# Attention's sum over eight keys: three additions on VectorE, or one strided reduction

## The chip, the cores and the metric

The kernel runs on one core of a Trainium2 chip. The metric is the device time of one execution in microseconds; beside the times stands the profile of one execution, with every instruction's start and duration. The engines are called by their names in the profile: PE (TensorE, matrix products; PEld is its loading of weights), DVE (VectorE), ACT (ScalarE), POOL (GpSimd) and SP (SyncE, which here issues transfers).

## What is computed

The input x has 2048 rows of 576 numbers in f32. Its normalized rows go through two branches, and the sum of both and of x is the output.

```python
xn = layernorm(x)
out = x + attention(xn, wqkv, wo) + ffn(xn, w1, b1, w2, b2)

# attention: 32 heads of 18 numbers; query s sees the 8 keys s, s-2, ..., s-14
logits = einsum("bhsd,bhswd->bhsw", q, kg) * 18**-0.5    # positions before 0 are masked
attn = softmax(logits)
o = einsum("bhsw,bhswd->bhsd", attn, vg)                 # the sum over w, the eight keys
return o.reshape(B, S, D) @ wo

# ffn, hidden width 4608
h = relu(xn @ w1 + b1) ** 2
return h @ w2 + b2
```

The change concerns the line marked "the sum over w".

## The kernel before, in words

The 2048 rows are four blocks b of 512 (`TB`), and in a block partition p holds the four neighbouring rows 4p to 4p + 3, called j. The 32 heads are four groups g of eight heads, so a group has 8 x 18 = 144 columns (`CG`).

PE carries most of the time. Its products are made exact enough by splitting each f32 operand in a high half, which ACT writes, and a low half, which DVE writes as the difference. The first product of the feed-forward part takes two blocks at a time and saves products by sums and differences of quarters of the matrices (slots T1, B11, B12 and so on). It is `ffn_pair` (lines 638 to 818), 18 pairs for each half s of the rows. Between its products PE does the second product of the pair before (`add`, line 557, with weights in the tiles w2s). In a pair, DVE adds a PSUM bank and an SBUF tile at lines 772 and 792, and PE goes on in the same bank `bc` after that.

The order of the work is: QKV products for the first rows, `phase_a(0)` (the pairs of blocks 0 and 1, and the second product of block 0), `phase_b0` (the second product of block 1, then the QKV products of blocks 2 and 3 by `quad_step`, whose `row` copies a PSUM bank by ACT and adds a second one by DVE, line 1105), `phase_a(1)` and `phase_b1` (the second product of the last block). In the phases b, DVE makes one low half of a w2 tile (`w2_lo`, line 538) for every 14 matmuls of PE; three tiles of w2s go round, and ACT (`w2_hi`, line 530) fills one when PE has done with it.

Attention has no phase of its own. `attention(b, g)` (lines 384 to 426) is a generator: one pass for each of the 16 pairs (b, g), cut in pieces by `yield`. `side(k)` (lines 430 to 445) runs the next k pieces, and the code above calls it at places that were put there by hand, so the order of DVE's instructions is fixed when the kernel is built. Each engine works through its own instructions in that order, whatever the times are.

A pass has keys k and values v as tiles with a halo of 14 earlier rows, so that the eight keys of row j are eight runs of 144 numbers, two rows apart (`shifted`, line 349). For each of the four j it multiplies q by the eight shifted keys into the tile `pr` (128 partitions, 8 x 144 numbers, line 391) and sums over 18 numbers of a head (line 395). Then come the softmax (lines 398 to 408) and, for each j, the second half: line 414 multiplies the weights by the shifted values into `pr`, a `yield`, and lines 417 to 419 sum `pr` over the eight keys into row j of the tile q, which is free by then. After the last j, POOL issues eight transfers of the rows to DRAM (line 424), and `release` (line 425) lets the next loads of keys and values go. `regroup` (line 884) later reads the rows back, and `o_hi` (line 903) transposes them on DVE for the product with wo.

Helpers record under their own line: every DVE operation of `tt` has L118, so the groups are told apart by tile and shape.

Of the kernel before, what the change touches and what calls it, by code (L numbers as in the profile page):

```python
# [12 lines left out]
ALU = mybir.AluOpType  # L13
ET = mybir.EngineType
AX = mybir.AxisListType
# [35 lines left out]
def block_kernel(ctx: ExitStack, tc: tile.TileContext, x, xt, wqkv, wo, w1, b1, w2, b2, w1l, out):  # L51
    nc = tc.nc
# [12 lines left out]
    def kv_tile(n):  # L65
# [25 lines left out]
                            axis=AX.XY, op=ALU.add)  # L91
# [25 lines left out]
    def tt(out, a, b, op):  # L117
        return nc.vector.tensor_tensor(out=out, in0=a, in1=b, op=op)  # L118
# [230 lines left out]
    def shifted(t, j, *dims):  # L349
        a = t[:, j:j + 1, 0:1]  # L350
        return bass.AP(tensor=a.tensor, offset=a.offset, ap=[a.ap[0], [DIL * CG, W], *dims])
# [19 lines left out]
    def release():  # L371
        free[0] += 1
        fetch()

    def offer(b, g=None):
        if g is None:
            loads.append(("x", b, None))
            queue.append((("x", b), lambda: statistics(b)))
        else:
            loads.extend([("k", b, g), ("v", b, g)])  # L380
            queue.append((("k", b, g), lambda: attention(b, g)))
        fetch()

    def attention(b, g):
        k, q = landed.pop(("k", b, g)), landed.pop(("q", b, g))
        lg = sb.tile([P, NA, W], F32, name="lg")
        mx = sb.tile([P, NA], F32, name="mx")
        sm = sb.tile([P, NA], F32, name="sm")
        for j in range(NJ):
            pr = sb.tile([P, W, CG], F32, name="pr")  # L390
            tt(pr, q[:, j:j + 1].to_broadcast([P, W, CG]), shifted(k, j, [1, CG]), ALU.mult)
            if j == NJ - 1:
                release()
            yield
            nc.vector.tensor_reduce(out=lg[:, j * HG:(j + 1) * HG].rearrange("p a w -> p w a"),  # L395
                                    in_=pr.rearrange("p w (a d) -> p w a d", d=DH), axis=AX.X, op=ALU.add)
            yield
        if b == 0:
            l4 = lg[:4].rearrange("p (j h) w -> p j h w", j=NJ)
            tt(l4, l4, mask[:4, :, None].to_broadcast([4, NJ, HG, W]), ALU.add)  # L400
        nc.vector.tensor_reduce(out=mx, in_=lg, axis=AX.X, op=ALU.max)
        tt(lg, lg, mx[:, :, None].to_broadcast([P, NA, W]), ALU.subtract)
        yield "exp"
        nc.scalar.activation(lg, lg, AF.Exp, scale=SCALE)
        yield
        nc.vector.tensor_reduce(out=sm, in_=lg, axis=AX.X, op=ALU.add)
        nc.vector.reciprocal(sm, sm)
        tt(lg, lg, sm[:, :, None].to_broadcast([P, NA, W]), ALU.mult)
        yield
        v = landed.pop(("v", b, g))  # L410
        for j in range(NJ):
            pr = sb.tile([P, W, CG], F32, name="pr")
            at = lg[:, j * HG:(j + 1) * HG].rearrange("p a w -> p w a")
            tt(pr.rearrange("p w (a d) -> p w a d", d=DH), at[:, :, :, None].to_broadcast([P, W, HG, DH]),
               shifted(v, j, [DH, HG], [1, DH]), ALU.mult)
            yield
            tt(pr[:, :4], pr[:, :4], pr[:, 4:], ALU.add)
            tt(pr[:, :2], pr[:, :2], pr[:, 2:4], ALU.add)
            tt(q[:, j], pr[:, 0], pr[:, 1], ALU.add)
            if j == NJ - 1:  # L420
                for k, (a, z) in enumerate(OPART):
                    rows = oscr[b, k][g * L:(g + 1) * L].rearrange("l (j i) c -> l i j c", i=G)
                    for i in range(G):
                        nc.gpsimd.dma_start(rows[:, i], q[i * L:(i + 1) * L, :, a:z])  # L424
                release()
            yield
# [1373 lines left out]
```

## Time and profile before

| what | value |
|---|---|
| median of 3 runs | 1105.33 us (1104.26 to 1106.77) |
| profiled execution | 1104.88 us |
| its span, first to last instruction | 1103.2 us |
| granted PE clock | 1.000 |
| PE busy | 1091.4 us (99%) |
| DVE busy | 889.3 us (81%) |
| ACT busy | 566.5 us (51%) |

The profile's page gives the busy time of each engine, the chain of work that ended last (followed back from the last instruction, at each step to what released it), and groups of instructions: line, engine, operation, output and input tiles, partitions x elements, count, then the total busy time in us, the mean of one in ns, and the engine's idle time before them. The views asked of the trace are such groups for a window, the waits of an engine, the chain in order of time, and the timeline: start, duration (several equal ones that follow each other are merged, "x2"), engine, line and operation, and in brackets the engine's idle time and what ended it.

### The profile page before, as it was taken

The page shows a single profiled execution, that of the slowest core. Times are in us where ns is not written, and L with a number is a line of the kernel's source. Part 1 is how long each engine was busy: PE and PEld are TensorE (multiplying, and loading weights), DVE is VectorE, ACT ScalarE, POOL GpSimd, SP SyncE. Part 2 cuts the span into 40 slices and gives each one's busy share as a digit, 9 for nine tenths or more (in the row PEclk, how much of TensorE's full clock was granted, in tenths as well). Part 3 has the DMA queues.
Part 4 walks back from the last instruction along what each step waited for, and adds up shares of the span by engine and source line. Part 5 has one row for each costly group of instructions (what it writes and reads, how often), then busy time and mean ns, then how long its engine had stood idle before and what let it go on. Part 6 is the DMA issues. An engine that isn't in the chain of part 4 may idle for free.

```text
span 1103.2 us, 13965 instructions
## 1 busy us (share of the span) xinstructions
PE 1091.4 (99%) x4919; PEld 918.8 (83%) x4919; DVE 889.3 (81%) x1197; ACT 566.5 (51%) x801; POOL 156.8 (14%) x284
## 2 busy tenths in 40 slices
PE   9999999999999999999999999999999999999998
PEld 7998888888888888888899887888888888888887
DVE  7996888999988979989899285776867676889955
ACT  5555655666656564555344354454554545543432
POOL 4011220212130100003010300202101010101010
PEclk9999999999999999999999999999999999999999
DMA  8768998897898697876865988868686877685582
GB/s 275 260 210 294 307 362 305 315 379 275 316 349 297 227 383 245 289 241 226 311 193 164 314 307 278 283 239 320 216 308 209 295 236 301 227 282 190 184 284 87
DMA packets 106549, 297.32 MB, mean 270 GB/s; under 512 B 12784, under 2 KB 39664, under 8 KB 95728
## 3 DMA queue, kind: packets, MB, share of 16 engines
q1 hardware_dynamic: 69104, 188.26, 49.1%
q0 software_dynamic: 14272, 67.24, 17.2%
q10 hardware_dynamic: 23104, 40.94, 11.1%
q8 instruction: 38, 0.62, 0.2%
q14 instruction: 31, 0.25, 0.1%
HBM read 211.90 MB, written 84.49 MB: 269 GB/s over the span
## 4 chain that ended last, share of the span: by engine, by line
PE 88%; DVE 6%; DMA 2%; issue 2%; ACT 1%; ACTq 1%; POOL 0%; DVEq 0%; POOLq 0%
PE p L557 45%; PE p L661 34%; PE p L1093 4%; DVE pr L118 2%; DMA w1s<-w 1%; PE p L1465 1%; PE p L1555 1%; PE p L1097 1%; DVE h L118 1%; DMA out<-h 1%; PE p L667 1%; PE p L1610 1%; DVE r L118 0%; PE p L1382 0%; DVE w1s L118 0%
## 5 line engine op out<-in xcount | busy, mean ns | idle before, releaser
L557 PE MATMUL p<-h,w2s 128*128 128x512 f32 x2066 | 491.9, 389 | 0.0
L557 PEld LDWEIGHTS p<-h,w2s 128*128 128x128 f32 x2066 | 387.6, 188 | 81.7 <-ACT h L708 0.5
L661 PE MATMUL p<-X,w1s 128*128 128x512 f32 x864 | 219.3, 389 | 0.0
L530 ACT ACTIVATE w2s<-w2r 128x640 fp32r<-128x640 f32 x164 | 120.3, 736 | 139.4 <-PE p L557 108.1
L661 PEld LDWEIGHTS p<-X,w1s 128*128 128x128 f32 x864 | 162.2, 188 | 33.7
L118 DVE TENSOR_TENSOR w2s<-w2r,w2s 128x576 fp32r<-128x576 f32 (+1 forms) x165 | 124.0, 752 | 77.2 <-ACT w2s L530 77.1
L661 PE MATMUL p<-S,w1s 128*128 128x512 f32 x648 | 164.8, 390 | 1.4 <-ACT r L746 1.4
L661 PEld LDWEIGHTS p<-S,w1s 128*128 128x128 f32 x648 | 121.5, 188 | 27.2 <-ACT r L746 1.8
L424 POOL DMA_DIRECT2D o<-q x128 | 69.5, 613 | 422.9 <-DVE q L118 421.8
L704 ACT ACTIVATE r<-r,b1t 128x512 f32<-128x512 f32 x72 | 52.2, 724 | 116.3 <-DVE r L118 113.6
L118 DVE TENSOR_TENSOR pr<-lg,kv 128x1152 f32<-128x1152 f32 x64 | 86.7, 1355 | 1.1
L395 DVE TENSOR_REDUCE lg<-pr 128x64 f32<-128x1152 f32 x64 | 86.5, 1351 | 1.2
L118 DVE TENSOR_TENSOR pr<-q,kv 128x1152 f32<-128x1152 f32 x64 | 86.7, 1354 | 0.9
L118 DVE TENSOR_TENSOR r<-p,r 128x512 f32<-128x512 f32 (+1 forms) x77 | 53.1, 690 | 35.5 <-ACT r L770 17.3
L118 DVE TENSOR_TENSOR pr<-pr 128x576 f32<-128x576 f32 (+1 forms) x128 | 77.6, 606 | 3.3
L712 ACT ACTIVATE r<-r 128x1024 f32<-128x1024 f32 x72 | 76.1, 1056 | 1.2
L746 ACT ACTIVATE r<-p 128x512 f32<-128x512 f32 x36 | 21.5, 598 | 84.2 <-PE p L661 81.1
L118 DVE TENSOR_TENSOR h<-r,h 128x1024 fp32r<-128x1024 f32 (+2 forms) x43 | 49.8, 1162 | 13.4 <-ACT r L712 9.6
L118 DVE TENSOR_TENSOR w1s<-w1r,w1s 128x1024 fp32r<-128x1024 f32 (+2 forms) x42 | 46.3, 1103 | 8.7 <-ACT w1s L495 8.2
L704 ACT ACTIVATE r<-p,b1t 128x512 f32<-128x512 f32 x72 | 48.2, 671 | 0.4 <-DMA out<-r 0.4
L118 DVE TENSOR_TENSOR h<-h 128x1024 fp32r<-128x1024 f32 x36 | 43.9, 1220 | 1.7 <-ACT h L989 1.5
L557 PE MATMUL p<-w1s,w2s 128*128 128x512 f32 x195 | 44.7, 389 | 0.0
(227 smaller groups left out, 1185.1 us busy)
## 6 DMA issues: line engine op xcount, KB each, us to landing
w2r<-in_w SPq DMA_DIRECT2D x144, 320.0 KB, 3.7
kv<-kvq POOLq DMA_DIRECT2D x32, 1296.0 KB, 8.2
w<-w1s SPq DMA_DIRECT2D x21, 1024.0 KB, 6.6
w1s<-w ACTq DMA_DIRECT2D x19, 1024.0 KB, 6.2
h<-r SPq DMA_DIRECT2D x36, 512.0 KB, 6.1
h<-h SPq DMA_DIRECT2D x36, 512.0 KB, 4.3
w<-w1s SPq DMA_DIRECT2D x15, 768.0 KB, 9.6
w1s<-w ACTq DMA_DIRECT2D x15, 768.0 KB, 5.6
```

What stands on the lines that cost most here:

```text
L118: return nc.vector.tensor_tensor(out=out, in0=a, in1=b, op=op)
L395: nc.vector.tensor_reduce(out=lg[:, j * HG:(j + 1) * HG].rearrange("p a w -> p w a"), in_=pr.rearrange("p w (a d) -> p w a d", d=DH), axis ...
L424: nc.gpsimd.dma_start(rows[:, i], q[i * L:(i + 1) * L, :, a:z])
L530: nc.scalar.activation(w2s[stream[i]][:, :DE], raw2[i], AF.Copy)
L557: nc.tensor.matmul(yp[b][c], v, a, start=c not in yb[b], stop=c in last and c not in [o[0] for o in ops[i + 1:]], skip_group_check=True)
L661: nc.tensor.matmul(to, l, r, start=start and i == 0, stop=i == len(mm) - 1, skip_group_check=True)
L667: nc.tensor.matmul(to, weight(LEFT, k, f), v, start=False, stop=k == 1, skip_group_check=True)
L704: nc.scalar.activation(to, a, AF.Relu, bias=b1t[:, f:f + 1])
L712: nc.scalar.activation(r, r, AF.Square)
L746: nc.scalar.activation(u[:, 0], bb, AF.Copy)
L1093: nc.tensor.matmul(to, l[:, js], r, start=start and n == 0, stop=n == len(mm) - 1, skip_group_check=True)
L1097: nc.tensor.matmul(to, v[:, js], ws[LEFT, f][:, n], start=False, stop=n == 1, skip_group_check=True)
```

## The change

Three additions that halve the eight keys, 8 to 4 to 2 to 1, become one reduction. It reads `pr` with the keys innermost: for each of the 144 columns the eight numbers that lie 144 words apart. The output is the same row of q. The pieces, the calls of `side` and all other instructions stay in their order.

```diff
             tt(pr.rearrange("p w (a d) -> p w a d", d=DH), at[:, :, :, None].to_broadcast([P, W, HG, DH]),
                shifted(v, j, [DH, HG], [1, DH]), ALU.mult)
             yield
-            tt(pr[:, :4], pr[:, :4], pr[:, 4:], ALU.add)
-            tt(pr[:, :2], pr[:, :2], pr[:, 2:4], ALU.add)
-            tt(q[:, j], pr[:, 0], pr[:, 1], ALU.add)
+            nc.vector.tensor_reduce(out=q[:, j], in_=pr.rearrange("p w c -> p c w"), axis=AX.X, op=ALU.add)
             if j == NJ - 1:
```

## Prediction

> **What bounds the kernel now.** I read first the page's head and its chain of work, then the waits of TensorE (PE), then VectorE's (DVE's) groups by shape.
>
> ```profile
> span 1103.2 us, 13965 instructions
> PE 1091.4 (99%) x4919; PEld 918.8 (83%) x4919; DVE 889.3 (81%) x1197; ACT 566.5 (51%) x801; POOL 156.8 (14%) x284
> PE 88%; DVE 6%; DMA 2%; issue 2%; ACT 1%; ACTq 1%; POOL 0%; DVEq 0%; POOLq 0%
> ```
>
> PE is busy for 1091.4 of 1103.2 us, so at most 11.8 us can be won anywhere. DVE, whose work is changed, is on 6% of the chain that ended last. A cheaper DVE pays only where PE waits for it; a dearer one is free until it has used up the time by which DVE runs ahead of PE, and from there each microsecond counts. So the question has two parts: what one strided sum costs, and how far ahead of PE DVE is at each place where the sums stand. Of PE's waits, one lies behind DVE's attention work:
>
> ```profile
> PE p L1093 <- ACT kv L1103: 0.9, 1, 0.9
> ```
>
> **What is removed and added.** There are 64 sums (16 passes of attention by 4 rows). Rows of DVE's groups by shape (busy us, mean ns of one | idle before):
>
> ```profile
> L118 DVE TENSOR_TENSOR pr<-pr 128x576 f32<-128x576 f32 x64 | 48.3, 754 | 1.1
> L118 DVE TENSOR_TENSOR pr<-pr 128x288 f32<-128x288 f32 x64 | 29.3, 458 | 2.2
> L118 DVE TENSOR_TENSOR q<-pr 128x144 f32<-128x144 f32 x64 | 19.7, 308 | 2.2
> L395 DVE TENSOR_REDUCE lg<-pr 128x64 f32<-128x1152 f32 x64 | 86.5, 1351 | 1.2
> L401 DVE TENSOR_REDUCE mx<-lg 128x32 f32<-128x256 f32 x16 | 6.7, 416 | 0.3
> L933 DVE TENSOR_SCALAR r<-r,flip 128x512 f32<-128x512 f32 x4 | 1.9, 486 | 3.0 <-ACT r L925 3.0
> ```
>
> Removed: 754 + 458 + 308 ns, and 2.2/64 us, or 34 ns, of idle before each of the last two: 1588 ns a sum, 101.6 us in all. Added: one TENSOR_REDUCE that reads 1152 elements and writes 144. L395 reads as many, in order, in 1351 ns; L401 has the new groups of eight, in order, at 416 ns for 256. Between the two rows an element costs (1351 - 416)/896 = 1.044 ns and an instruction 149 ns.
>
> What no row shows is the order of the reads: in the new sum successive elements lie 144 words apart, and no operand of DVE in this trace steps so. **Lower end**: the order costs nothing, 1351 ns as L395. Below that I see no way, since every element is still read. **Upper end**: each element takes two turns, 149 + 1152 x 2.088 = 2554 ns. **My value**: L933 takes its contiguous words at (486 - 149)/512 = 0.658 ns each, so words that lie side by side can come in together. I assume that a word without a neighbour behind it wastes such an access, and charge every element one on top of its own 1.044: 149 + 1152 x 1.702 = 2109 ns. That is an assumption. I take it because L395, the lower end, has neighbours throughout and the new sum has none, so the lower row is the one that is far. With d for what a sum adds to DVE's time: d = -0.24 us at the lower end, 0.52 at my value, 0.97 at the upper end.
>
> The row of L395 alone would make the change a gain. [...]
>
> **Where a dearer sum reaches PE.** DVE works in program order; behind a longer sum stand its other jobs: freeing PSUM banks, and the low halves of weights. A lag grows by d with every sum and is gone when DVE next waits for PE.
>
> Place 1, the first of the QKV products of phase b0, in the chain of waits (start us, us, what):
>
> ```profile
> 541.59 1.36 DVE h L969 x2
> ...
> 550.14 0.77 DVE pr L118
> ...
> 554.73 0.68 DVE pr L118
> ...
> 558.05 0.77 DVE pr L118
> ...
> 561.62 0.77 DVE pr L118
> ...
> 572.95 1.06 DVE w1r L118
> ...
> 574.03 0.02 ACT w1s L1025
> ...
> 574.87 0.52 ACT kv L1103
> ```
>
> From 541.59 to the weights at 572.95 the chain is DVE's; four sums stand in it (a row each for their first addition). ACT's split of these weights, and its copy at 574.87 behind it in its queue, hold PE: this is the wait of 0.9 us above. No room is left, so **4d = 2.08 us**.
>
> Place 2, the pair of phase a0 at 176 to 190 us (start, duration, engine):
>
> ```profile
> 175.89 1.25 DVE L118 TENSOR_TENSOR pr<-pr 128x576 f32<-128x576 f32 x2
> 181.61 1.25 DVE L118 TENSOR_TENSOR pr<-pr 128x576 f32<-128x576 f32 x2
> 184.64 1.25 DVE L118 TENSOR_TENSOR pr<-pr 128x576 f32<-128x576 f32 x2
> 188.62 0.69 DVE L118 TENSOR_TENSOR r<-p,r 128x512 f32<-128x512 f32 x1
> 189.61 1.52 PE L661 MATMUL p<-X,w1s 128*128 128x512 f32 x6
> ```
>
> Line 772 reads bank bc until 188.62 + 0.69 = 189.31; PE goes on in that bank at 189.61. Three sums and a room of 0.30: **3d - 0.30 = 1.26 us**.
>
> Place 3, the pair at 362 to 382:
>
> ```profile
> 362.34 0.69 DVE L118 TENSOR_TENSOR r<-p,r 128x512 f32<-128x512 f32 x1 [0.38 <-ACT r L770]
> 363.95 1.24 DVE L118 TENSOR_TENSOR pr<-pr 128x576 f32<-128x576 f32 x2
> 367.44 1.24 DVE L118 TENSOR_TENSOR pr<-pr 128x576 f32<-128x576 f32 x2
> 373.17 1.24 DVE L118 TENSOR_TENSOR pr<-pr 128x576 f32<-128x576 f32 x2
> 381.33 0.68 DVE L118 TENSOR_TENSOR r<-p,r 128x512 f32<-128x512 f32 x1
> 382.19 1.09 PE L661 MATMUL p<-X,w1s 128*128 128x512 f32 x4
> ```
>
> The same with a room of 382.19 - 382.01 = 0.18: **3d - 0.18 = 1.38 us**. The first row also shows the usual pair: DVE waits there (0.38 us), and has more room; those pairs, with one or two sums each, I cost at nothing, the cover being that wait and PE's seven matmuls of L557 that follow.
>
> Place 4, the last part of the QKV products:
>
> ```profile
> 593.95 1.24 DVE L118 TENSOR_TENSOR pr<-pr 128x576 f32<-128x576 f32 x2
> 597.37 1.24 DVE L118 TENSOR_TENSOR pr<-pr 128x576 f32<-128x576 f32 x2
> 600.78 1.24 DVE L118 TENSOR_TENSOR pr<-pr 128x576 f32<-128x576 f32 x2
> 603.67 0.60 DVE L118 TENSOR_TENSOR st<-p,st 128x432 f32<-128x432 f32 x1
> 604.33 4.86 PE L1093 MATMUL p<-w1s,S 128*128 128x432 f32 x24
> ```
>
> Line 1105 frees a bank at 604.27; I take it that the second six of PE's 24 matmuls need it, at 604.33 + 6 x 4.86/24 = 605.55. Three sums, room 1.28: **3d - 1.28 = 0.28 us**.
>
> Place 5, phase b1, where DVE splits every w2 tile. Groups of the window 986 to 1047.6, and the timeline at its end:
>
> ```profile
> L118 DVE TENSOR_TENSOR w2s<-w2r,w2s 128x576 fp32r<-128x576 f32 x21 | 15.7, 751 | 1.1 <-ACT w2s L530 1.1
> L118 DVE TENSOR_TENSOR q<-pr 128x144 f32<-128x144 f32 x8 | 2.5, 308 | 0.3
> ```
>
> ```profile
> 1046.73 1.42 DVE L118 TENSOR_TENSOR w2s<-w2r,w2s 128x576 fp32r<-128x576 f32 x2
> 1049.60 0.74 ACT L530 ACTIVATE w2s<-w2r 128x640 fp32r<-128x640 f32 x1 [1.49 <-PE p L557]
> 1052.78 0.74 ACT L530 ACTIVATE w2s<-w2r 128x640 fp32r<-128x640 f32 x1 [2.43 <-PE p L557]
> ```
>
> The idle 1.1 us opens the window; then eight sums follow with no wait for PE, and the lag reaches 8d. The first of the two splits ends at 1046.73 + 0.75 = 1047.48. ACT takes that tile's buffer again at 1052.78, when PE has done its 14 matmuls; a tile takes 1052.78 - 1049.60 = 3.18 us, and the low half is needed from the fifth of the 14 on, 2.27 us before the end, at some 1050.5. Room 3.0: **8d - 3.0 = 1.17 us**.
>
> Sum: 10d - 0.48 for places 1 to 3 and the two terms that open later; at d = 0.52 it is 2.08 + 1.26 + 1.38 + 0.28 + 1.17 = **6.2 us**. The profiled execution took 1104.88 us (span 1103.2 and 1.7 around it), 0.45 under the median of three runs, so 1111.1 on its own footing and **1111.5** on that of the median 1105.33. Output and load DMAs behind each pass's last sum, which GpSimd issues when DVE is done, move with the lag; I cost them at nothing. The cover is that the rows are read back a phase later. If it were gone, behind the pass of place 4, it would be up to 4d = 2.1 us.
>
> **Rivals.** (1) The order of the reads costs nothing. For it: L395 and L401, whose groups of 18 and of 8 cost the same per element. [...] Then d = -0.24, DVE saves 15 us in all, and PE gets only place 1: 4 x 0.24, or the wait of 0.9 there: 1104.4 us, no change. (2) The sum is dear, but the rooms at places 2 to 5 are larger than I read them, since I infer them from the next matmul in the bank: place 1 alone, 1107.4, within the bound. It decides as long as the lag of three sums, 1.6 us, is covered in both pairs. (3) DVE becomes the bound: were an element to take three turns (149 + 1152 x 3.132 = 3757 ns, d = 2.17), the same five terms give 8.7 + 6.2 + 6.3 + 5.2 + 14.4 = 41 us, and 1146 us. Against it: no row hints at such a price. That the change doesn't do what it says I leave out: it is one instruction in place of three.
>
> **How the numbers follow.** 0.2%, about what a measurement of this kernel can tell from no change, is 2.2 us; places 1 to 3 pass it at d = 0.27, a sum of 1.86 us. Forecast (a sum between 1.86 and 2.55 us, mostly uncovered) 0.64; rival 1, 0.19; rival 2, 0.08; rival 3, 0.06; a gain of over 2.2 us by some way that I don't see, 0.03. Faster 0.03, same 0.27, slower 0.70. The upper end gives 3.9 + 2.6 + 2.7 + 1.6 + 4.8 = 15.6 us, 1120.9; the forecast alone runs from 1107.5 to 1121, and with rivals 1 and 2 the range is 1103.9 to 1121, which leaves out a tenth.
>
> **What would show it.** The mean of the new group (q<-pr, 128x144<-128x1152): 2.1 us by the forecast, 1.35 by rival 1, over 3 by rival 3. PE's waits: new ones on DVE's r<-p,r and on w2s, near 190, 382 and 1005 to 1050 us, and the one at 574 us grown from 0.9 to some 3 us. The forecast is wrong if the group's mean is under 1.86 us, or if it is dear and PE's busy share stays 99% with no such waits.

## Result and the profile after

| | before | after |
|---|---|---|
| median, 4 runs each beside one another | 1105.84 us (1104.26 to 1106.77) | 1113.22 us (1111.70 to 1117.14) |
| ratio after / before | | 1.0069 (95%: 1.0047 to 1.0092) |
| profiled execution | 1104.88 us | 1117.14 us |

The change makes the kernel slower by 7.4 us between the medians. The profiled execution of the kernel after is the slowest of its four, 12.3 us above that of before, so places read from its trace add up to more than the medians show; a second profile, further down, says which of them come back.

From the page of the kernel after (line numbers behind 417 are two lower than before): span, busy time of the engines, the chain that ended last, and the new sum's group.

```profile
span 1115.4 us, 13837 instructions
PE 1096.5 (98%) x4919; PEld 919.7 (82%) x4919; DVE 927.6 (83%) x1069; ACT 567.1 (51%) x801; POOL 155.3 (14%) x284
PE 67%; DVE 17%; DMA 8%; issue 5%; ACT 2%; POOL 1%; ACTq 0%; SPq 0%; DVEq 0%; POOLq 0%
L417 DVE TENSOR_REDUCE q<-pr 128x144 f32<-128x1152 f32 x64 | 139.4, 2178 | 1.1
```

A sum takes 2178 ns where three additions took 1588, so d is 0.59 us by these rows. DVE has 128 instructions fewer and is busy for 38 us more. That is 0.60 us a sum, but busy time leaves out the idle time between instructions, which the prediction's d counts; read where DVE runs through eight sums without a wait (under Experiments), d is 0.58 us. DVE's share of the chain went from 6% to 17%, though it is busy for only 83% of the span: the added time counts where PE's next work stands behind DVE.

PE's waits in the kernel after (in all, times, longest):

```profile
PE p L659 <- DVE r L118: 3.6, 3, 1.4
PE p L665 <- DMA w1s<-w: 3.5, 1, 3.5
PE p L1091 <- ACT p L1115: 2.7, 1, 2.7
PE p L555 <- DVE w2s L118: 1.1, 3, 0.5
```

The first and the last row are new, on the two tiles that the prediction named. The third is place 1. The second stood at 1.7 us before and was not foreseen. PE's timeline of the kernel after shows where they are:

```profile
190.63 1.66 PE L659 MATMUL p<-X,w1s 128*128 128x512 f32 x6 [1.42 <-DVE r L118]
...
349.75 1.66 PE L659 MATMUL p<-X,w1s 128*128 128x512 f32 x6 [0.96 <-DVE r L118]
...
386.35 1.66 PE L659 MATMUL p<-X,w1s 128*128 128x512 f32 x6 [1.27 <-DVE r L118]
...
683.71 2.68 PE L555 MATMUL p<-h,w2s 128*128 128x512 f32 x7
...
1058.53 3.50 PE L555 MATMUL p<-h,w2s 128*128 128x512 f32 x14 [0.48 <-DVE w2s L118]
```

190.63 is place 2, 386.35 place 3, 1058.53 place 5. How such a wait comes about is seen in DVE's timeline at place 2: the last sum ends at 187.50, the addition that frees PE's bank at 190.58, and PE goes on at 190.63.

```profile
181.70 2.18 DVE L417 TENSOR_REDUCE q<-pr 128x144 f32<-128x1152 f32 x1
185.31 2.19 DVE L417 TENSOR_REDUCE q<-pr 128x144 f32<-128x1152 f32 x1
...
189.90 0.68 DVE L118 TENSOR_TENSOR r<-p,r 128x512 f32<-128x512 f32 x1
```

To see what each place costs, I set the start of PE's n-th matmul in one trace against the start of the n-th in the other: PE has the same 4919 matmuls in the same order, so a step in the difference is time lost there, whatever the cause. The steps of the kernel after against before, in us, at the times of the kernel before: place 2, 1.7; 348 us, 1.3; place 3, 1.5; 406 us, 0.4; place 1, 4.5 with matmuls that run slowly behind the wait, of which 1.6 come back by 591; place 4, nothing; 627 us, -1.7 (a wait of 1.4 on ACT in the kernel before is gone); 648 us, 0.5; 675 us, 3.3 with slow matmuls; 951 us, 0.5; place 5, 2.0. With -0.2 of small steps that makes the 12.2 us between the two spans. The steps that the prediction named come to 8.1 us, and the others to the rest.

### The profile page after: what moved, and what is told of

It reads as the page before. It is cut to its first block, busy times and chain, and to the rows that moved or that the text cites. A ratio compares the mean times of both kernels' runs of the same rounds, so it can differ in the third digit from the quotient of the medians.

```text
span 1115.4 us, 13837 instructions
## 1 busy us (share of the span) xinstructions
PE 1096.5 (98%) x4919; PEld 919.7 (82%) x4919; DVE 927.6 (83%) x1069; ACT 567.1 (51%) x801; POOL 155.3 (14%) x284
## 4 chain that ended last, share of the span: by engine, by line
PE 67%; DVE 17%; DMA 8%; issue 5%; ACT 2%; POOL 1%; ACTq 0%; SPq 0%; DVEq 0%; POOLq 0%
PE p L555 31%; PE p L659 24%; PE p L1091 6%; DVE pr L118 3%; DVE q L417 3%; DVE h L118 2%; DVE w2s L118 2%; DVE w1s L118 2%; DMA w1s<-w 1%; PE p L1095 1%; DVE r L118 1%; DMA w2r<-in_wo 1%; DVE lg L395 1%; PE p L1463 1%; DMA lw<-st 1%
## 5 line engine op out<-in xcount | busy, mean ns | idle before, releaser
L555 PE MATMUL p<-h,w2s 128*128 128x512 f32 x2066 | 494.3, 390 | 1.4 <-DVE w2s L118 0.9
L555 PEld LDWEIGHTS p<-h,w2s 128*128 128x128 f32 x2066 | 387.4, 188 | 85.4 <-DVE w2s L118 2.2
L417 DVE TENSOR_REDUCE q<-pr 128x144 f32<-128x1152 f32 x64 | 139.4, 2178 | 1.1
L118 DVE TENSOR_TENSOR h<-r,h 128x1024 fp32r<-128x1024 f32 (+2 forms) x43 | 49.6, 1157 | 10.6 <-ACT r L710 9.6
L555 PE MATMUL p<-w1s,w2s 128*128 128x512 f32 x195 | 44.7, 389 | 0.0
## 6 DMA issues: line engine op xcount, KB each, us to landing
w<-w1s SPq DMA_DIRECT2D x15, 768.0 KB, 10.6
```

The source lines that it names most:

```text
L417: nc.vector.tensor_reduce(out=q[:, j], in_=pr.rearrange("p w c -> p c w"), axis=AX.X, op=ALU.add)
L555: nc.tensor.matmul(yp[b][c], v, a, start=c not in yb[b], stop=c in last and c not in [o[0] for o in ops[i + 1:]], skip_group_check=True)
```

## Experiments

Every edit is made to the kernel after, at line 417 unless it says otherwise; added lines without a removed one beside them stand in place of that line. Each was compared with the kernel before in runs on the same chip. d, what a sum adds to the time that it holds DVE, is read in phase b1, from DVE's row of h ahead of the eight sums to its split behind them: DVE waits for no other engine between the two, they are 1046.73 - 986.76 = 59.97 us apart in the kernel before, and d is what that stretch grows by, over 8. "The formula" is the prediction's sum of places: 10d - 0.48, and, where they are above nothing, 3d - 1.28 and 8d - 3.0.

**What makes the sum dear: its order of reading.** The same instruction, with the same number of reads and outputs, adds eight neighbours:

```diff
-nc.vector.tensor_reduce(out=q[:, j], in_=pr.rearrange("p w c -> p c w"), axis=AX.X, op=ALU.add)
+nc.vector.tensor_reduce(out=q[:, j], in_=pr.rearrange("p w (c k) -> p (w c) k", k=W), axis=AX.X, op=ALU.add)
```

> The reduction keeps its 1152 elements and 144 groups of eight but reads them in the order in which they lie, so it adds eight neighbouring numbers in place of the eight keys (this part of the computation is changed). If the order of the reads is what costs, its mean falls from 2178 ns to that of L395, 1351 ns, VectorE has 15 us less to do than before the change, and the time is 1104 to 1106 us, within 0.2% of before: only the wait near 574 us can shrink, by at most 1 us. If 144 groups or the reduction itself cost more, the mean stays near 2178 ns and the time near 1113 us.

Measured 1102.75 us against 1104.74, ratio 0.9986 (0.9974 to 0.9998). The page's head and the group:

```profile
PE 1090.9 (99%) x4919; PEld 918.7 (83%) x4919; DVE 878.2 (80%) x1069; ACT 566.5 (51%) x801; POOL 155.1 (14%) x284
L417 DVE TENSOR_REDUCE q<-pr 128x144 f32<-128x1152 f32 x64 | 86.3, 1349 | 1.1
```

1349 ns against 2178 with nothing changed but the order: all of the loss comes from the stride, none from the reduction as such. It also shows what a cheaper sum is worth. DVE is 11 us less busy and the kernel gains some 2 us, since PE hardly waits for DVE. The wait of PE on kv at place 1 is gone, as rival 1 had it, and PE starts 1.1 us earlier from there on; another 0.5 us is won at 542 us, where I had named no wait.

**Which steps are dear.** One execution with sixteen orders of the 1152 reads, one for each block and row, four sums each, so that most sums hold other numbers:

```diff
+at_step = lambda s: (q[:, j, :s], flat.rearrange("p (n s) -> p s n", s=s), AX.X)
+runs = lambda r: (q[:, j, :CG // r], pr.rearrange("p w (c r) -> p c w r", r=r), AX.XY)
+odd = (q[:, j, :CG // 2 - 1], pr[:, :, 1:CG - 1].rearrange("p w (c r) -> p c w r", r=2), AX.XY)
...
+    nc.vector.tensor_reduce(**total(*at_step(24)))
```

> Sixteen forms of the reduction over the same tile, one for each block and row, most of which add up other numbers than the eight keys (that part of the computation is changed): steps of 2, 4, 8, 16, 24, 36, 48, 72, 96, 128 and 144 words, and runs of 2, 3 and 4 neighbours 144 words apart, and of 2 that begin on an odd word. If what costs is a word without a neighbour behind it, runs of 2 and 4 take 1351 ns like reads in order, and every step from 2 up costs some 2.2 us. If the distance is what costs, small steps are cheap and the price grows with the step, and runs do not help much. The whole time is not of interest.

Some of the groups by shape; the number of outputs (128x2 and so on) is the step in words in the first seven rows, then come runs of 2, of 4 and of 3 neighbours, and pairs that begin on an odd word:

```profile
L424 DVE TENSOR_REDUCE q<-pr 128x2 f32<-128x1152 f32 x4 | 5.4, 1352 | 0.1
L426 DVE TENSOR_REDUCE q<-pr 128x4 f32<-128x1152 f32 x4 | 8.8, 2191 | 0.1
L428 DVE TENSOR_REDUCE q<-pr 128x8 f32<-128x1152 f32 x4 | 9.6, 2396 | 0.1
L430 DVE TENSOR_REDUCE q<-pr 128x16 f32<-128x1152 f32 x4 | 8.4, 2102 | 0.1
L432 DVE TENSOR_REDUCE q<-pr 128x24 f32<-128x1152 f32 x4 | 12.1, 3017 | 0.1
L436 DVE TENSOR_REDUCE q<-pr 128x72 f32<-128x1152 f32 x4 | 9.7, 2428 | 0.0
L442 DVE TENSOR_REDUCE q<-pr 128x144 f32<-128x1152 f32 x4 | 8.7, 2176 | 0.1
L444 DVE TENSOR_REDUCE q<-pr 128x72 f32<-128x1152 f32 x4 | 5.4, 1349 | 0.1
L446 DVE TENSOR_REDUCE q<-pr 128x36 f32<-128x1152 f32 x4 | 5.4, 1350 | 0.1
L450 DVE TENSOR_REDUCE q<-pr 128x48 f32<-128x1152 f32 x4 | 5.5, 1366 | 0.1
L448 DVE TENSOR_REDUCE q<-pr 128x71 f32<-128x1136 f32 x4 | 6.8, 1702 | 0.1
```

Any step from 4 words on costs 56% or more (2102 ns and up, against 1349 in order), and runs of two or four neighbours are free though they lie 144 words apart (1349 and 1350 ns). But a step of 2 words is free too (1352 ns), which the prediction's picture (a word without a neighbour behind it wastes an access) does not give. Runs of three cost next to nothing, (1366 - 149)/1152 = 1.06 ns an element. Pairs that begin on an odd word take (1702 - 149)/1136 = 1.37 ns, nearly half of the way from the 1.04 ns in order to the 1.76 at a step of 144. The rows give these prices and no more: why a step of 2 is free, why the odd start costs, and why the longer steps differ among each other is not shown.

**Can the stride be moved to the multiplication?** Line 414 writes the products with the eight keys of a column side by side, and the sum reads in order:

```diff
+by_column = pr.rearrange("p w c -> p (w c)").rearrange("p (c w) -> p c w", w=W)
-tt(pr.rearrange("p w (a d) -> p w a d", d=DH), at[:, :, :, None].to_broadcast([P, W, HG, DH]),
+tt(by_column.rearrange("p (a d) w -> p w a d", d=DH), at[:, :, :, None].to_broadcast([P, W, HG, DH]),
...
-nc.vector.tensor_reduce(out=q[:, j], in_=pr.rearrange("p w c -> p c w"), axis=AX.X, op=ALU.add)
+nc.vector.tensor_reduce(out=q[:, j], in_=by_column, axis=AX.X, op=ALU.add)
```

> The multiplication of line 414 writes its products with the eight keys of a column side by side, so that the reduction reads in order and the multiplication writes 8 words apart. If the price lies in the step on whichever side has it, the reduction falls to 1351 ns and the multiplication rises from 1354 ns by at least as much as the reduction had paid, 0.8 us: 1112 us or more. If only reads pay, the multiplication stays at 1354 ns and the time is within 0.2% of before.

Measured 1115.54 us against 1105.87, ratio 1.0103 (1.0086 to 1.0121). Multiplication and sum:

```profile
L118 DVE TENSOR_TENSOR pr<-lg,kv 128x1152 f32<-128x1152 f32 x64 | 153.8, 2403 | 1.1
L418 DVE TENSOR_REDUCE q<-pr 128x144 f32<-128x1152 f32 x64 | 86.2, 1347 | 1.1
```

The sum is cheap, but the multiplication, 1355 ns before, takes 2403: a write at a step of 8 words costs as much as the read at that step above (2396). The stretch of eight sums takes 65.80 us, so d = 0.73.

**Half the stride on each side.** The steps say that 2 words are free (1352 ns) and that runs of two from an even word on are free (1349 ns). So the multiplication writes two keys of a column side by side (a write at a step of 2), and the sum reads pairs:

```diff
+paired = pr.rearrange("p w c -> p (w c)").rearrange("p (u c t) -> p u c t", c=CG, t=2)
-tt(pr.rearrange("p w (a d) -> p w a d", d=DH), at[:, :, :, None].to_broadcast([P, W, HG, DH]),
-   shifted(v, j, [DH, HG], [1, DH]), ALU.mult)
+a0 = v[:, j:j + 1, 0:1]
+v5 = bass.AP(tensor=a0.tensor, offset=a0.offset, ap=[a0.ap[0], [2 * DIL * CG, W // 2], [DIL * CG, 2], [DH, HG], [1, DH]])
+at5 = lg[:, j * HG:(j + 1) * HG].rearrange("p a (u t) -> p u t a", t=2)
+tt(paired.rearrange("p u (a d) t -> p u t a d", d=DH), at5[:, :, :, :, None].to_broadcast([P, W // 2, 2, HG, DH]), v5, ALU.mult)
...
-nc.vector.tensor_reduce(out=q[:, j], in_=pr.rearrange("p w c -> p c w"), axis=AX.X, op=ALU.add)
+nc.vector.tensor_reduce(out=q[:, j], in_=paired.rearrange("p u c t -> p c u t"), axis=AX.XY, op=ALU.add)
```

> The multiplication of line 414 writes keys 2u and 2u+1 of a column side by side (a step of 2 words in its writes), and one reduction adds the four such pairs, which lie 288 words apart. In the table of steps, reads in runs of 2 and reads at a step of 2 words took the time of reads in order. If writes go by the same rule, the multiplication stays at 1354 ns, the reduction takes 1351 ns, a sum is 0.24 us shorter than the three additions, and the time is 1 to 2 us under before, as with the reads in order. If a write at a step of 2 words pays like one at 8 (2403 ns), it is some 9 us over before.

Measured 1102.96 us against 1105.65, ratio 0.9974 (0.9963 to 0.9985): below both kernels. Multiplication and sum:

```profile
L118 DVE TENSOR_TENSOR pr<-lg,kv 128x1152 f32<-128x1152 f32 x64 | 86.8, 1356 | 1.1
L421 DVE TENSOR_REDUCE q<-pr 128x144 f32<-128x1152 f32 x64 | 86.3, 1349 | 1.1
```

Neither pays anything for its order, and one instruction replaces three after all. The gain is small for the reason that the prediction gave: DVE is 11 us less busy, but PE waits for it in few places. Which waits the 2.7 us come from is not settled: the profiled execution of this kernel is the slowest of its ten (1105.38 us), and this is among PE's waits in it:

```profile
PE p L663 <- DVE r L118: 1.2, 1, 1.2
```

The bank at the end of a pair can be late even with a cheap sum.

**Where the loss arises.** The strided sum in some of the four blocks, the three additions in the others (`b == 1` and `b > 1` in the second and third kernel):

```diff
+if b == 0:
     nc.vector.tensor_reduce(out=q[:, j], in_=pr.rearrange("p w c -> p c w"), axis=AX.X, op=ALU.add)
+else:
+    tt(pr[:, :4], pr[:, :4], pr[:, 4:], ALU.add)
+    tt(pr[:, :2], pr[:, :2], pr[:, 2:4], ALU.add)
+    tt(q[:, j], pr[:, 0], pr[:, 1], ALU.add)
```

> The strided sum only in the passes of block 0, three additions in the others. My theory, with d = 0.59 us a sum: place 2 gives 3d - 0.30 = 1.5 us, and the late transfer behind line 188 near 348 us, seen in the changed kernel's trace, 1.2 us more: 2 to 3.5 us over before. If PE pays at place 1 alone: no change.

> The strided sum only in the passes of block 1, three additions in the others. My theory: place 3 (its sums are those of the pass of block 1 that comes first) 3d - 0.18 = 1.6 us, the wait near 410 us 0.4, place 1 4d = 2.4 us, and place 4 up to 0.5: 4 to 5 us over before, and up to 1.5 more if the granted clock falls behind a long wait of PE, as it did in the changed kernel's trace. If PE pays at place 1 alone: 2.4 us.

> The strided sum only in the passes of blocks 2 and 3, three additions in the others. My theory: phase a1 has room for two sums a pair, phase b1 has room for 3.0 us of the eight sums' lag of 8d = 4.7: 1.7 us over before. If the first phase were as tight as the pairs of phase a0: over 4 us. If PE pays at place 1 alone: no change.

Measured against 1104.74 us: block 0 alone 1107.08, ratio 1.0022 (1.0008 to 1.0036); block 1 alone 1107.30, 1.0024 (1.0013 to 1.0035); blocks 2 and 3 alone 1106.88, 1.0023 (1.0011 to 1.0036). The three excesses add up to 0.69%, the whole change's 0.69%; each is uncertain by some 0.13%, so this says that the blocks carry the loss between them, and not how exactly. PE's waits that are new, block 0:

```profile
PE p L664 <- DVE r L118: 2.1, 1, 2.1
```

block 1:

```profile
PE p L1096 <- ACT p L1120: 2.6, 2, 2.3
...
PE p L664 <- DVE r L118: 1.3, 1, 1.3
```

blocks 2 and 3:

```profile
PE p L560 <- DVE w2s L118: 1.9, 4, 0.7
```

Each block brings the waits of its own places: block 0 the pair of place 2 (a step of 2.2 us, and 1.8 of slow matmuls behind it), block 1 place 3 (1.5) and place 1 (2.4), blocks 2 and 3 place 5 (3.7). Block 1 lost 2.7 us (1.4 to 3.9) and not the 4 to 5 expected; in its trace 1.7 us come back at 627 us, where I had counted nothing. Its time alone would also fit a loss at place 1 only; the step at place 3 in its trace tells the two apart. The trace of blocks 2 and 3 also has a wait of 0.87 us at place 2, where its sums are the old three additions. So the room of 0.30 us that I read there varies by more than itself from one execution to the next. Block 0 alone has no step at 348 us: that one needs more than block 0's sums, or doesn't come every time.

**Is it only DVE's time, or the access too?** Here the edit is made to the kernel before. The three additions stay, and a fourth on columns that are read no more adds DVE time in order:

```diff
 tt(pr[:, :4], pr[:, :4], pr[:, 4:], ALU.add)
 tt(pr[:, :2], pr[:, :2], pr[:, 2:4], ALU.add)
 tt(q[:, j], pr[:, 0], pr[:, 1], ALU.add)
+dead = pr[:, 4:].rearrange("p w c -> p (w c)")[:, :390]
+tt(dead, dead, dead, ALU.add)
```

> The three additions of before, and behind them one more addition of 390 columns on VectorE whose result nobody reads: 149 + 390 x 1.044 + 34 = 590 ns, so that a sum holds VectorE as long as the strided one does, with all reads in order. If only VectorE's time counts, the kernel takes as long as the changed one on the same chip, 1111 to 1117 us, with PE waits at the same places. If the strided reads also disturb others through SBUF, it stays clearly below, at 1108 us or less.

Measured 1110.19 us against 1105.87, ratio 1.0044 (1.0028 to 1.0061). The added instruction:

```profile
L118 DVE TENSOR_TENSOR pr<-pr 128x390 f32<-128x390 f32 x64 | 35.7, 558 | 0.0
```

The dose was too small: 558 ns long, it starts before its predecessor has ended (at 182.82 us in its timeline, where the row's last addition ends at 182.90), and the stretch of eight sums takes 63.80 us, so d = 0.48. At that d the formula gives 5.3 us, the medians differ by 4.3, and the run doesn't tell the theories apart. So once more with 486 columns, beside the change itself on the same chip:

> As the run with 390 dead columns, with 486: there the dead addition started before its forerunner had ended, and so added less to VectorE's time than its own length. 149 + 486 x 1.044 = 656 ns, less some 0.07 us of overlap, is the 0.59 us of the strided sum. If VectorE's time is all that counts, this kernel and the changed one, both on this chip, agree within their intervals. If strided reads cost something beside, it stays 2 us or more below the changed one.

> The changed kernel itself, on the same chip as the run with 486 dead columns: some 1.0069 times before, as in its first comparison.

Measured against 1105.65 us: 486 columns 1111.61, ratio 1.0054 (1.0041 to 1.0066); the change again 1113.93, ratio 1.0070 (1.0050 to 1.0090). The ends of the stretch of eight sums, before (its second end is shown in the prediction):

```profile
986.76 1.23 DVE L118 TENSOR_TENSOR h<-h 128x1024 fp32r<-128x1024 f32 x1 [0.19 <-ACT h L989]
```

with 486 columns:

```profile
989.61 1.23 DVE L118 TENSOR_TENSOR h<-h 128x1024 fp32r<-128x1024 f32 x1 [0.19 <-ACT h L991]
...
1054.19 1.42 DVE L118 TENSOR_TENSOR w2s<-w2r,w2s 128x576 fp32r<-128x576 f32 x2
```

the change again:

```profile
994.87 1.23 DVE L118 TENSOR_TENSOR h<-h 128x1024 fp32r<-128x1024 f32 x1 [0.19 <-ACT h L987]
...
1059.48 1.43 DVE L118 TENSOR_TENSOR w2s<-w2r,w2s 128x576 fp32r<-128x576 f32 x2
```

The stretch takes 64.58 us with 486 columns and 64.61 in the change, against 59.97: d = 0.58 in both, so the doses are equal. The medians differ by 2.3 us, more than the 2 that I had set as the sign of a cost beside DVE's time, but the intervals overlap. Such a cost isn't shown, and one of some 2 us isn't excluded. Two figures hint at where to look. PE's wait for w1s at 675 us, 1.7 us before, is 1.6 us with 486 columns and 1.1 in the kernel with the strided write; it is over 3 us only in the two profiles of the change. And the share of the PE clock that was not granted, times the span, comes by estimate to 1.6 us on average in the 15 runs of before, 1.8 in the 5 with 486 columns and 3.0 in the 6 of the change.

The change's second profile (the run took 1114.98 us) has these among PE's waits:

```profile
PE p L665 <- DMA w1s<-w: 3.1, 1, 3.1
PE p L659 <- DVE r L118: 2.7, 3, 1.3
...
PE p L1091 <- DVE h L967: 1.9, 1, 1.9
...
PE p L555 <- DVE w2s L118: 0.9, 2, 0.5
```

Places 2, 3 and 5 come back (steps of 1.5, 1.5 and 2.0 us), the transfer at 675 us too (1.4), and -1.3 at 627. The step at 348 us shrinks to 0.5. In place 1's stretch the time now goes at 542 us (0.7, and 1.5 of slow matmuls) and at 570 (0.7).

All doses together (us over before: by the formula at the measured d, and by the ratio):

| kernel | d | formula | measured (95%) |
|---|---|---|---|
| 390 columns more | 0.48 | 5.3 | 4.9 (3.1 to 6.7) |
| 486 columns more | 0.58 | 7.4 | 6.0 (4.5 to 7.3) |
| the change | 0.58 | 7.4 | 7.6 (5.2 to 10.2) |
| the change again | 0.58 | 7.4 | 7.7 (5.5 to 9.9) |
| strided write | 0.73 | 10.6 | 11.4 (9.5 to 13.4) |

A loss in plain proportion, 13 us for each microsecond of d, meets these rows about as well, so the table bears out the size of the loss and not the form of the formula.

## Why the prediction was right, point by point

- **What bounds the kernel.** Right: a dearer DVE counts only where its lead is used up. That the loss grows with d faster than in proportion, as rooms open, isn't shown.
- **The price of a sum.** The direction was right, the size a little low: 2178 ns against 2109, so d = 0.58 and not 0.52. This is the term that was mis-sized. It is worth 1.2 us (the same formula gives 6.2 us at 0.52 and 7.4 at 0.58) of the 1.7 between forecast (1111.5) and result (1113.2); the other 0.5 is the median of before, 1105.84 beside the result and 1105.33 in the forecast. The reason assumed for the price was not quite it: at a step of 2 words, too, no word is followed by its neighbour, and that sum took 1352 ns, as in order. An element of the new sum took (2178 - 149)/1152 = 1.76 ns, where 1.70 had been assumed; what makes it cost that is not shown.
- **Place 1** (4d = 2.3 at 0.58): 2.4 us with block 1 alone, some 2.9 net in the first profile, slow matmuls among them. The wait is another than the one I named. ACT's copy of kv (0.9 us before) is gone in the first profile, and PE waits some twenty matmuls earlier, 2.7 us on ACT's p of L1115.
- **Places 2 and 3** (1.4 and 1.6 at 0.58): 1.7 and 1.5 in the first profile, 1.5 and 1.5 in the second. Right, though place 2's room is no fixed number.
- **Place 4** (0.5 at 0.58): nothing. The step that failed is the room of 1.28 us, read from the trace before as if PE's place in time were fixed. PE had itself been held at place 1, 30 us earlier, and came later by more than DVE. In the timeline of the kernel after, DVE's row that frees the bank ends at 609.66, and PE's 24 matmuls, the second six of which need it, begin only at 611.99:

```profile
609.06 0.60 DVE L118 TENSOR_TENSOR st<-p,st 128x432 f32<-128x432 f32 x1
```

```profile
611.99 4.86 PE L1091 MATMUL p<-w1s,S 128*128 128x432 f32 x24
```

- **Place 5** (1.6 at 0.58): 2.0 and 2.0, on the tile named, but 3.7 with blocks 2 and 3 alone. This room is no fixed number either.
- **What I left out.** DMAs behind the lag were costed at nothing, and in the first profile PE loses time behind two transfers. At 675 us its wait for w1s grew from 1.7 to 3.5 us. At 348 us POOL's output transfers and load of kv ran later (from 318.06 and 323.65 us on, 314.71 and 320.14 before), POOL's own small operation behind them held a transpose on DVE (326.76, before 323.42), the load of st went out 2.7 us later on SP's queue, DVE waited 2.8 us for it, and PE lost 1.3. Two rows of the timeline of the kernel after:

```profile
333.20 0.72 SPq L608 DMA_DIRECT2D st<-in_w1l  x1
...
342.69 1.27 DVE L118 TENSOR_TENSOR st<-st 128x128 f32<-128x128 f32 x4 [2.82 <-DMA st<-in_w1l]
```

  Against them stand -1.7 at 627 us, where PE had waited for ACT anyway, and the 1.6 that came back at place 1. Slow matmuls behind a wait are not in the sum either. That the formula meets the difference of the medians, 7.4 us, so closely is in part luck: in the two profiled executions of the change the spans are 12.2 and 10.1 us longer than before's, some 8 of each at the places named.
- **The rivals.** Rival 1 (the order costs nothing) falls by the row of 2178 ns, and the kernel that reads in order shows what it would have brought: 0.9 us of gain by my working, 1.5 (0.2 to 2.9) by the measured ratio. Rival 2 (place 1 alone) falls by block 0 and by blocks 2 and 3, which lose without place 1. Rival 3 (DVE becomes the bound) falls by the mean of the sums.

Open: why the transfer at 675 us comes later, whether the chain through POOL's queue at 348 us is the cause of that step or only goes with it (no kernel took either away), whether strided reads cost something beside DVE's time, and where exactly the 2.7 us of the paired kernel come from.

## What to carry to other kernels

Count what an instruction reads in what order, not how many instructions there are: three additions in order beat one reduction over keys that lie far apart, 1588 to 2178 ns. Where a reduction must run over an outer dimension, let the producer write two of its values side by side; here both instructions then took the time of those in order (1356 and 1349 ns). And a room in front of a wait is read from one execution: it moves with the engine that waits, so a place behind an earlier wait may cost nothing, as place 4 did, while rooms of a few tenths of a microsecond, as at places 2 and 3, are better counted as none.

## What the runs showed of the hardware that I had not expected

- The price of a step is not even. Per element, less the 149 ns of an instruction: 1.04 ns at a step of 2 words, 1.77 at 4, 1.95 at 8, 1.70 at 16, 2.49 at 24 (3017 ns), 1.98 at 72 and 1.76 at 144.
- Behind some of PE's longer waits the matmuls run slowly for a while. After the wait of 3.46 us at 683 us, seven matmuls of L555 took 2.68 us, where seven take 1.75. The granted clock (the figure before the last two) fell in the windows of 25 us around both such places of this trace, at 578 and 683 us; the kernel before:

```profile
575.00:600.00 25.00, 24.25 (x122) 22.98 (x123) 23.73 (x32) 12.71 (x24) 1.08 (x2) 1.00 0.56 172
675.00:700.00 25.00, 25.00 (x110) 20.69 (x111) 17.14 (x24) 11.36 (x16) 4.36 (x8) 1.00 0.75 255
```

and the kernel after:

```profile
575.00:600.00 25.00, 22.40 (x105) 21.10 (x106) 22.86 (x29) 13.22 (x24) 2.29 (x5) 0.93 0.61 193
675.00:700.00 25.00, 21.54 (x88) 17.37 (x87) 14.85 (x15) 10.25 (x15) 0.00 (x0) 0.93 0.72 235
```

Each time some 1.5 to 1.8 us are lost beside the wait itself, about what a granted clock of 0.93 leaves out of 25 us (1.75). Waits of 1.9 us (the change again) and 2.1 us (block 0 alone) had this behind them, those of 2.3 us (block 1 alone), 2.5 us (the strided write) and 3.1 us (the change again, at 683 us) had not (granted clock of the profiled execution: 0.998 in the change again and with block 0 alone, 1.000 with block 1 alone and in the strided write), so the length of the wait alone doesn't decide it.
